# The last four expert tiles moved into three conditional blocks

## The chip, the cores and the metric

The kernel runs on one core of a Trainium2 chip. The metric is the device time of one execution in microseconds (us). A core has five engines that run side by side and wait for each other by semaphores: TensorE (PE in the profile; PEld is its weight loading), VectorE (DVE), ScalarE (ACT), GpSimd (POOL) and SyncE (SP). SP mostly issues transfers (DMA) here.

## The reference

Two things are computed, one after the other. First a Fourier filter along the sequence of 8 batches, then a mixture of 8 experts in which the token's number decides the expert:

```python
# x: (8, 2496, 256) float32; filt_r, filt_i: (1249, 256)
X = np.fft.rfft(x, axis=1)
y = np.fft.irfft(X * (filt_r + 1j * filt_i)[None], n=2496, axis=1)

x = y.reshape(19968, 256)
expert_idx = token_ids * np.int64(2654435761) % np.int64(8)
for e in range(8):
    mask = expert_idx == e
    h = np.maximum(x[mask] @ w1[e], 0.0)      # w1[e]: 256 x 1024
    out[mask] = h @ w2[e]                      # w2[e]: 1024 x 256
```

Everything is float32. The inputs are drawn from a fixed seed; the token numbers are drawn evenly from 0 to 49999.

## The kernel before

The tokens are sorted by expert into tiles of 128 rows, each tile of one expert. A tile that an expert doesn't fill is padded with blank rows. How many tiles are needed depends on the data: the sum over the experts of the number of tokens, divided by 128 and rounded up. The kernel is written for the worst case, 163 tiles, and always runs all of them; tiles beyond the needed number hold blank rows alone, and their results are scattered to a row index out of range, which drops them.

```python
TB = 128
NT = (N + E * (TB - 1)) // TB          # 163
STAGES = (2, 4, 6, 8)                  # a tile of stage g needs the filter's output of the first STAGES[g] batches

def stage_tiles():
    ends = [(S * b - E * (TB - 1)) // TB // 2 * 2 for b in STAGES[:-1]] + [NT]   # 30, 70, 108, 163
    out, first = [], 0
    for end in ends:
        half = (end - first + 1) // 2
        out.append([first + i // 2 + (half if i % 2 else 0) for i in range(end - first)])
        first = end
    return out
```

A stage's tiles are run alternately from its first and from its second half, so that the even steps use one pair of weight buffers and the odd steps the other. The weights of step i+2 are asked for in step i; the transfer is conditional (`cond`) on the expert being another than two steps before:

```python
    def weights(i, which):
        if i >= NT:
            return
        if i >= 2 and which == 0:
            ws[i] = ws[i - 2]
        eng, kw = nc.gpsimd if i < 2 else nc.sync, {}
        e = eng.value_load(chunk_i[0:1, 0, i:i + 1], ...)
        if i >= 2:
            kw = {"cond": eng.value_load(chunk_i[0:1, 1, i:i + 1], ...)}
        # which 0: w1 of expert e, 1 MB, into ws[i][0]; which 1: w2, 1 MB, into ws[i][1]
        eng.dma_start(..., **kw)
```

`rv["last"]` is the running sum of the tiles made, by stage and expert; its last element is the number of tiles that are needed. The expert of each tile and the flag of a change are worked out in `experts()` and left in `chunk_i`.

The main loop, with the pieces that it calls:

```python
    xps = pool(ctx, "xps", 1, PSUM)         # one buffer for the transposes
    work = pool(ctx, "work", 2)
    outs = pool(ctx, "outs", 3)

    def turn(i):                            # transposes of tile i's rows
        ps = xps.tile([P, DP, TB], F32, ...)
        for dp in range(DP):                # 2
            nc.tensor.transpose(out=ps[:, dp, :], in_=xg[i][:, dp * P:(dp + 1) * P], identity=ident[:])
        xt[i] = work.tile([P, DP, TB], F32, ...)
        nc.vector.tensor_copy(out=xt[i][:], in_=ps[:])

    def up(i, ht):                          # 16 matmuls 128x128x128, relu on ACT (quad 0) and DVE (quad 1)
        ...
    def down(i, ht):                        # 8 matmuls 128x128x256, then:
        ...
        o = outs.tile([P, C], F32, name=f"osb_{i}", tag="osb")
        nc.vector.tensor_copy(out=o[:], in_=ps[:])
        st = nc.gpsimd.indirect_dma_start(  # scatter of the tile's rows to out
            out=out[:], out_offset=..., in_=o[:], in_offset=None, bounds_check=N - 1, oob_is_err=False)

    for i in range(4):
        load(i)                             # gather buffer xg[i] <- xs
    turn(0)
    for i in range(NT):
        ht = work.tile([P, FP, TB], F32, name=f"ht_{i}", tag="ht")
        if i + 4 < NT:
            load(i + 4)
        up(i, ht)
        weights(i + 2, 0)
        if i + 1 < NT:
            turn(i + 1)
        while main and main[0][0] < i + 1:  # pieces of the filter for the later batches, up to step 101
            main.pop(0)[1]()
        down(i, ht)
        weights(i + 2, 1)
```

Of the kernel before, what the change touches and what calls it, by code (L numbers as in the profile page):

```python
# [11 lines left out]
F32 = mybir.dt.float32  # L12
I32 = mybir.dt.int32
# [6 lines left out]
P = 128  # L20
B, S, C = 8, 2496, 256
N = B * S
E, F = 8, 1024
# [19 lines left out]
TB = 128  # L43
NT = (N + E * (TB - 1)) // TB
W = C + 16
NJ = N // P
DP = C // P
FP = F // P
STAGES = (2, 4, 6, 8)
G = len(STAGES)  # L50
NPAD = NT * TB - N
NQP = NPAD // P


def stage_tiles():


    ends = [(S * b - E * (TB - 1)) // TB // 2 * 2 for b in STAGES[:-1]] + [NT]
    out, first = [], 0
    for end in ends:  # L60
        half = (end - first + 1) // 2
        out.append([first + i // 2 + (half if i % 2 else 0) for i in range(end - first)])
        first = end
    return out


# [30 lines left out]
def route_table():  # L97


    t = np.zeros((P, G + 2 + NQP + HN + 1), np.float32)  # L100
    p = np.arange(P)
    r = np.arange(NR)
    t[:NR, G + 2 + NQP:] = (N2 * (r % N1) + np.array(H0)[r // N1])[:, None] + np.arange(HN + 1)
    for g, b in enumerate(STAGES):
        t[:, g] = p < b * S // NJ
    order = sum(stage_tiles(), []) + [NT] * (2 * P - NT)
    t[:, G:G + 2] = np.array(order).reshape(2, P).T
    t[:, G + 2:G + 2 + NQP] = p[:, None] * NQP + np.arange(NQP)
    return t
# [3 lines left out]
def kernel(  # L113
# [10 lines left out]
    nc = tc.nc  # L124
# [9 lines left out]
    def pool(stack, name, bufs, space=None):  # L134
        kw = {} if space is None else {"space": space}
        return stack.enter_context(tc.tile_pool(name=name, bufs=bufs, **kw))

    ctx.enter_context(tc.manual_schedule())
    keep = pool(ctx, "keep", 1)
# [4 lines left out]
    t2pool = pool(ctx, "t2", 4)  # L144
# [10 lines left out]
    sidx = keep.tile([NR, B, HN + 1], I32)  # L155
    tokno = keep.tile([NR, HN + 1], F32)
    chunk_i = keep.tile([1, 2, NT], I32)
    wf_t = cpool.tile([NR, NK], F32)
    wi_t = cpool.tile([NK, NR], F32)
    d_t = cpool.tile([P, NS, P], F32)  # L160
# [153 lines left out]
# [7 lines that stand above are left out]
        e = eng.value_load(chunk_i[0:1, 0, i:i + 1], min_val=0, max_val=E - 1)  # L321
        if i >= 2:
            kw = {"cond": eng.value_load(chunk_i[0:1, 1, i:i + 1], min_val=0, max_val=1)}
        if which == 0:
            eng.dma_start(out=ws[i][0][:], in_=moe_w1[bass.ds(e, 1)].rearrange("one (dp p) f -> p (one dp) f", p=P), **kw)
        else:
            eng.dma_start(out=ws[i][1][:], in_=moe_w2[bass.ds(e, 1)].rearrange("one (fp p) d -> p (one fp) d", p=P), **kw)
# [9 lines left out]
    nc.scalar.dma_start(tok[:], tok_h.bitcast(I32).rearrange("(p j two) -> p j two", p=P, two=2))  # L337
    rt = rpool.tile([P, G + 2 + NQP + HN + 1], F32)
    nc.scalar.dma_start(out=rt[:], in_=r_dram.ap())
    nc.vector.tensor_copy(tokno[:], rt[0:NR, G + 2 + NQP:])  # L340

# [47 lines left out]
    rv = {}  # L389
# [111 lines left out]
    def blanks():  # L501
# [10 lines left out]
        nc.vector.tensor_sub(prior[:], prior[:], pads[:])  # L512
        some = rpool.tile([P, NQP, E], F32)
        number = rt[:, G + 2:G + 2 + NQP]
# [16 lines left out]
    def experts():  # L531
        seg = rv["seg"]
        ps = fps.tile([P, 2, C], F32, name="ce_ps", tag="f")
        for q in range(2):
            nc.tensor.matmul(out=ps[0:1, 0, q * P:(q + 1) * P], lhsT=seg[:, q:q + 1], rhs=ident[:],
                             start=True, stop=True)
        ce = rpool.tile([1, 2 * P], F32)
        nc.vector.tensor_copy(ce[:], ps[0:1, 0, :])
        new = rpool.tile([1, NT], F32)
        nc.vector.memset(new[:, 0:2], 1.0)  # L540
        nc.vector.tensor_tensor(new[:, 2:], ce[:, 2:NT], ce[:, 0:NT - 2], op=OP.not_equal)
        nc.vector.tensor_copy(chunk_i[:, 0, :], ce[:, 0:NT])
        nc.vector.tensor_copy(chunk_i[:, 1, :], new[:])

# [15 lines left out]
    def part3(b, at, ready):  # L562
        bt = batches[b]
        return ([(at[u], lambda u=u: bt.stage3(u)) for u in range(NU)] +
                [(max(at[2 * v] - 2.5 * (at[1] - at[0]), ready), lambda v=v: bt.load4(v)) for v in range(NV)])

    order = stage_tiles()
    tiles = sum(order, [])
    stage_of = [g for g, o in enumerate(order) for _ in o]
# [8 lines left out]
    todo += part2(0, spaced(-128, -95, N_2), -142)  # L578
    todo += part1(1, spaced(-123.5, -105, NU), [-141.5, -135, -134.5])
    todo += [(-125, tile_experts), (-121, experts), (-108, blanks)]  # L580
    todo += [(-110, lambda: nc.sync.dma_start(out=wi_t[:], in_=wi_dram.ap()))]
    todo += [(-118.2 + .1 * i, lambda i=i: (weights(i, 0), weights(i, 1))) for i in range(2)]
# [21 lines left out]
    work = pool(ctx, "work", 2)  # L604
    outs = pool(ctx, "outs", 3)
    xg, xt = {}, {}

    def load(i):
        q = tiles[i]
        xg[i] = gath.tile([P, W], F32, name=f"xg_{i}", tag="xg")  # L610
        ld = nc.sync.dma_start(out=xg[i][:], in_=xs[q * TB:(q + 1) * TB, :])
        for b in range(STAGES[stage_of[i]], B):
            tc.declare_no_dep(ld.ins, group=f"xs_{b}", reason="the tiles of a stage hold tokens of its batches alone")
        tc.add_to_no_dep_group("xs_read", ld.ins)

    def turn(i):
        ps = xps.tile([P, DP, TB], F32, name=f"xps_{i}", tag="xps")
        for dp in range(DP):
            nc.tensor.transpose(out=ps[:, dp, :], in_=xg[i][:, dp * P:(dp + 1) * P], identity=ident[:])  # L619
        xt[i] = work.tile([P, DP, TB], F32, name=f"xt_{i}", tag="xt")  # L620
        nc.vector.tensor_copy(out=xt[i][:], in_=ps[:])  # L621

    def up(i, ht):
        w1 = ws[i][0]
        for quad in range(FP // 4):
            ps = ups.tile([P, 4, TB], F32, name=f"ups_{i}_{quad}", tag="ups")
            for k in range(4):
                fp = 4 * quad + k
                for dp in range(DP):
                    nc.tensor.matmul(out=ps[:, k, :], lhsT=w1[:, dp, fp * P:(fp + 1) * P],  # L630
                                     rhs=xt[i][:, dp, :], start=(dp == 0), stop=(dp == DP - 1))
            dst = ht[:, 4 * quad:4 * quad + 4, :]
            if quad % 2 == 0:
                nc.scalar.activation(out=dst, in_=ps[:], func=AF.Relu)  # L634
            else:
                nc.vector.tensor_scalar_max(dst, ps[:], 0.0)  # L636

    def down(i, ht):
        w2 = ws[i][1]
        ps = dps.tile([P, C], F32, name=f"dps_{i}", tag="dps")  # L640
        for fp in range(FP):
            nc.tensor.matmul(out=ps[:], lhsT=ht[:, fp, :], rhs=w2[:, fp, :],  # L642
                             start=(fp == 0), stop=(fp == FP - 1))
        o = outs.tile([P, C], F32, name=f"osb_{i}", tag="osb")
        nc.vector.tensor_copy(out=o[:], in_=ps[:])  # L645
        st = nc.gpsimd.indirect_dma_start(  # L646
            out=out[:], out_offset=bass.IndirectOffsetOnAxis(ap=xg[i][:, C:C + 1].bitcast(I32), axis=0),
            in_=o[:], in_offset=None, bounds_check=N - 1, oob_is_err=False)
        tc.declare_no_dep(st.ins, group="out_rows", reason="distinct rows")
        tc.add_to_no_dep_group("out_rows", st.ins)  # L650
        del xg[i]

    for i in range(4):
        load(i)
    turn(0)
    for i in range(NT):
        ht = work.tile([P, FP, TB], F32, name=f"ht_{i}", tag="ht")
        if i + 4 < NT:
            load(i + 4)
        up(i, ht)  # L660
        weights(i + 2, 0)
        if i + 1 < NT:
            turn(i + 1)
        while main and main[0][0] < i + 1:
            main.pop(0)[1]()
        down(i, ht)
        weights(i + 2, 1)
    assert not main


# [26 lines left out]
```

## Time and profile before

The time before is 1637.09 us, the median of three runs (1634.4 to 1637.64). The profiled execution took 1631.37 us, and its recorded span is 1629.8 us.

| stretch of the span, us | PE busy, us | DVE busy, us | POOL busy, us | DMA share |
|---|---|---|---|---|
| 0 to 400 | 309.02 | 178.42 | 102.79 | 0.70 |
| 400 to 700 | 293.81 | 113.93 | 73.00 | 0.66 |
| 700 to 1000 | 297.26 | 116.79 | 73.32 | 0.55 |
| 1000 to 1300 | 298.13 | 66.11 | 62.85 | 0.40 |
| 1300 to 1500 | 200.00 | 39.52 | 27.20 | 0.25 |
| 1500 to 1620 | 120.00 | 23.86 | 15.54 | 0.20 |
| 1620 to 1630 | 0.58 | 0.42 | 0.97 | 0.03 |

How to read it: each row is one stretch of time. Where an engine's busy time equals the length of the stretch, it had no gap. DMA share is the mean busy share of the core's 16 DMA engines. The first matmul of the expert tiles starts at 207.7 us, the last at 1620.2 us; between about 208 and 1100 us the filter of the later batches is worked in between the tiles, and after that the tiles run alone.

### The profile page before, as it was taken

Reading aid. Unit: us, or ns where it says so; the run is one execution under the profiler, and the core shown is the slowest. Engines: PE = TensorE matmul, PEld = TensorE weight load, DVE = VectorE, ACT = ScalarE, POOL = GpSimd, SP = SyncE. Lnnn points to the kernel's source line nnn. Section 1 sums busy time; section 2 is a strip of 40 time slices with the busy share of each in tenths; the row PEclk is TensorE's granted clock in tenths of the full one; section 3 lists DMA queues with packets and bytes.
Section 4 is the critical chain, followed back from the end, with each engine's and each line's share of the span. In section 5 each row is a group of like instructions: output and inputs, shape, how many; then the busy total and the mean of one; then the engine's idle time right before and its main releaser. Section 6 shows DMA issues by size and latency. Waiting matters only on the chain.

```text
span 1629.8 us, 26685 instructions
## 1 busy us (share of the span) xinstructions
PE 1518.8 (93%) x9522; PEld 1381.7 (85%) x9522; DVE 539.0 (33%) x1022; ACT 217.1 (13%) x371; POOL 355.7 (22%) x375
## 2 busy tenths in 40 slices
PE   3676589999999999999999999999999999999997
PEld 2554378988888999899989998999999999999997
DVE  6572142452244444233434442222122121221221
ACT  2322212112111111111111111000000000000000
POOL 0235300331320132122121322233111111111111
PEclk9788699999999999999999999999999999999999
DMA  7998627747864883674537643544152413132220
GB/s 189 306 290 244 198 98 205 240 165 207 245 218 150 244 256 111 194 197 147 185 114 222 199 135 115 147 127 162 45 203 79 140 37 126 52 94 88 84 84 9
DMA packets 152541, 258.77 MB, mean 159 GB/s; under 512 B 16185, under 2 KB 118508, under 8 KB 150410
## 3 DMA queue, kind: packets, MB, share of 16 engines
q1 hardware_dynamic: 103345, 163.46, 33.1%
q0 software_dynamic: 21136, 50.96, 9.4%
q10 hardware_dynamic: 27928, 42.65, 8.3%
q8 instruction: 76, 1.25, 0.3%
q14 instruction: 56, 0.45, 0.1%
HBM read 431.87 MB, written 86.09 MB: 318 GB/s over the span
## 4 chain that ended last, share of the span: by engine, by line
PE 42%; issue 36%; POOL 7%; DMA 3%; DVE 2%; POOLq 1%; ACT 0%; SPq 0%; ACTq 0%; DVEq 0%
PE ups L630 15%; PE dps L642 15%; POOL out_dram L646 6%; PE pb L240 3%; PE pa L203 3%; PE pc L263 3%; PE pd L203 2%; POOL xs L301 2%; DMA xs<-o,sidx 1%; PE xps L619 1%; DVE z L250 1%; PE pa L198 0%; POOLq L646 0%; DMA d<-g 0%; DVE y L247 0%
## 5 line engine op out<-in xcount | busy, mean ns | idle before, releaser
L630 PEld LDWEIGHTS ups<-xt,w 128*128 128x128 f32 x5216 | 610.3, 193 | 9.2 <-DVE xt L621 1.0
L630 PE MATMUL ups<-xt,w 128*128 128x128 f32 x5216 | 611.1, 276 | 0.6 <-DVE xt L621 0.6
L642 PE MATMUL dps<-w,ht 128*128 128x256 f32 x2608 | 591.0, 380 | 0.0
L642 PEld LDWEIGHTS dps<-w,ht 128*128 128x128 f32 x2608 | 490.0, 191 | 63.7 <-issue 1.6
L646 POOL DMA_INDIRECT out_dram<-osb,xg x163 | 159.6, 979 | 944.6 <-DVE osb L645 919.4
L636 DVE TENSOR_SCALAR ht<-ups 128x512 f32<-128x512 f32 x163 | 112.8, 692 | 526.8 <-PE ups L630 519.7
L634 ACT ACTIVATE ht<-ups 128x512 f32<-128x512 f32 x163 | 97.3, 597 | 1008.0 <-PE ups L630 992.3
L301 POOL DMA_INDIRECT xs<-o,sidx x176 | 175.3, 996 | 245.7 <-DVE o L205 145.7
L645 DVE COPY osb<-dps 128x256 f32<-128x256 f32 x163 | 69.3, 425 | 404.5 <-PE dps L642 396.2
L240 PE MATMUL pb<-t,d_t 128*128 128x256 f32 x320 | 91.1, 413 | 23.8 <-DMA t<-d 23.3
L250 DVE TENSOR_TENSOR z<-pb,filt 64x512 f32<-64x512 f32 x160 | 110.1, 688 | 2.2
L263 PE MATMUL pc<-y,e_t 128*128 128x256 f32 x320 | 90.1, 407 | 19.7 <-DVE y L251 19.3
L240 PEld LDWEIGHTS pb<-t,d_t 128*128 128x128 f32 x320 | 63.5, 209 | 35.5 <-issue 25.9
L263 PEld LDWEIGHTS pc<-y,e_t 128*128 128x128 f32 x320 | 63.3, 203 | 35.8 <-issue 17.5
L203 PE MATMUL pd<-t,wi_t 120*117 120x256 f32 x320 | 81.2, 399 | 11.7 <-DMA t<-d 7.1
L203 PEld LDWEIGHTS pd<-t,wi_t 120*117 120x117 f32 x320 | 58.9, 191 | 25.5 <-issue 9.1
L247 DVE TENSOR_TENSOR y<-pb,filt 128x512 f32<-128x512 f32 x80 | 55.3, 691 | 68.3 <-PE pb L240 67.8
L266 ACT COPY g<-pc 128x512 f32<-128x512 f32 x80 | 46.8, 585 | 233.2 <-PE pc L263 229.8
L621 DVE COPY xt<-xps 128x256 f32<-128x256 f32 x163 | 67.6, 415 | 1.9 <-PE xps L619 1.9
L619 PE MATMUL xps<-ident,xg 128*128 128x128 f32 x326 | 62.6, 274 | 3.1 <-DMA xg<-xs 3.1
L203 PE MATMUL pa<-x,wf_t 117*120 117x256 f32 x264 | 63.3, 383 | 0.6 <-DVE z L250 0.6
L205 ACT COPY t<-pa 120x512 f32<-120x512 f32 x80 | 46.0, 588 | 90.6 <-PE pa L203 88.1
(102 smaller groups left out, 352.5 us busy)
## 6 DMA issues: line engine op xcount, KB each, us to landing
w<-in_moe_w_dram SPq DMA_DIRECT2D x322, 1024.0 KB
xg<-xs SPq DMA_DIRECT2D x163, 136.0 KB
t<-d SPq DMA_DIRECT2D x80, 256.0 KB
d<-g ACTq DMA_DIRECT2D x80, 256.0 KB
d<-t ACTq DMA_DIRECT2D x16, 960.0 KB
t<-d SPq DMA_DIRECT2D x16, 960.0 KB
x<-in_x_dram SPq DMA_DIRECT2D x39, 312.0 KB
x<-in_x_dram SPq DMA_DIRECT2D x21, 234.0 KB
```

The costliest lines, as they stand in the source:

```text
L203: nc.tensor.matmul(out=ps[0:cols * H, k, :], lhsT=w[:], rhs=src[:, 2 * i + k, :], start=True, stop=True)
L240: nc.tensor.matmul(out=ps[:, i, :], lhsT=d_t[:, s, :], rhs=self.t2[s // SG][:, s % SG, :], start=True, stop=True)
L250: nc.vector.tensor_tensor(out=z[b], in0=ps[a], in1=f_t[1][a, sl, :], op=OP.mult)
L263: nc.tensor.matmul(out=ps[:, i, :], lhsT=e_t[:, 2 * u + i, :], rhs=pr[:, i, :], start=True, stop=True)
L301: st = nc.gpsimd.indirect_dma_start(out=xs[:], out_offset=bass.IndirectOffsetOnAxis(ap=index, axis=0), in_=rows, in_offset=None, bounds_ch ...
L619: nc.tensor.transpose(out=ps[:, dp, :], in_=xg[i][:, dp * P:(dp + 1) * P], identity=ident[:])
L630: nc.tensor.matmul(out=ps[:, k, :], lhsT=w1[:, dp, fp * P:(fp + 1) * P], rhs=xt[i][:, dp, :], start=(dp == 0), stop=(dp == DP - 1))
L634: nc.scalar.activation(out=dst, in_=ps[:], func=AF.Relu)
L636: nc.vector.tensor_scalar_max(dst, ps[:], 0.0)
L642: nc.tensor.matmul(out=ps[:], lhsT=ht[:, fp, :], rhs=w2[:, fp, :], start=(fp == 0), stop=(fp == FP - 1))
L645: nc.vector.tensor_copy(out=o[:], in_=ps[:])
L646: st = nc.gpsimd.indirect_dma_start(out=out[:], out_offset=bass.IndirectOffsetOnAxis(ap=xg[i][:, C:C + 1].bitcast(I32), axis=0), in_=o[:], ...
```

## The change

The number of needed tiles is copied into an integer and loaded into a register of every engine in step 151. The last four tiles (159 to 162) are taken out of the alternating order of the last stage and stand at its end. Their transposes are done unconditionally, into one buffer of their own (`spare`, in a pool of the filter that is free by then). The rest of their work stands in three conditional blocks: tile 159, tile 160, and tiles 161 with 162, each block run only if more tiles are needed than its first tile's number. The change is for leaving out tiles that hold nothing but blanks.

```diff
+NSURE = NT - 4
...
-    ends = [(S * b - E * (TB - 1)) // TB // 2 * 2 for b in STAGES[:-1]] + [NT]
+    ends = [(S * b - E * (TB - 1)) // TB // 2 * 2 for b in STAGES[:-1]] + [NSURE]
     out, first = [], 0
     ...
+    out[-1] += range(NSURE, NT)
     return out
...
+    used_i = keep.tile([1, 1], I32)
...
         nc.vector.tensor_copy(chunk_i[:, 1, :], new[:])
+        nc.vector.tensor_copy(used_i[:], rv["last"][0:1, G * E - 1:])
...
-    def turn(i):
+    def turn(i, to=None):
...
-        xt[i] = work.tile([P, DP, TB], F32, name=f"xt_{i}", tag="xt")
-        nc.vector.tensor_copy(out=xt[i][:], in_=ps[:])
+        xt[i] = work.tile([P, DP, TB], F32, name=f"xt_{i}", tag="xt")[:] if to is None else to
+        nc.vector.tensor_copy(out=xt[i], in_=ps[:])
...
-    for i in range(NT):
+    used = []
+
+    def step(i):
         ht = work.tile([P, FP, TB], F32, name=f"ht_{i}", tag="ht")
         if i + 4 < NT:
             load(i + 4)
         up(i, ht)
         weights(i + 2, 0)
-        if i + 1 < NT:
+        if i + 1 < NSURE:
             turn(i + 1)
         while main and main[0][0] < i + 1:
             main.pop(0)[1]()
         down(i, ht)
         weights(i + 2, 1)
+
+    for i in range(NSURE):
+        if i == NSURE - 8:
+            used.append(nc.values_load(used_i[0:1, 0:1], min_val=0, max_val=NT))
+        step(i)
     assert not main
+
+    spare = t2pool.tile([P, NT - NSURE, DP, TB], F32, name="spare", tag="t2")
+    for i in range(NSURE, NT):
+        turn(i, spare[:, i - NSURE])
+    for some in (range(NSURE, NSURE + 1), range(NSURE + 1, NSURE + 2), range(NSURE + 2, NT)):
+        with tc.If(used[0] > some[0]):
+            for i in some:
+                ht = work.tile([P, FP, TB], F32, name=f"ht_{i}", tag="ht")
+                up(i, ht)
+                weights(i + 2, 0)
+                down(i, ht)
+                weights(i + 2, 1)
```

## The prediction

> **What bounds the kernel now.** I read the page's shares and slices first, then its groups, then the timeline of the last tiles, and last the tail, by the instructions of the kernel's closing line. From the page:
>
> ```profile
> PE 1518.8 (93%) x9522; PEld 1381.7 (85%) x9522; DVE 539.0 (33%) x1022; ACT 217.1 (13%) x371; POOL 355.7 (22%) x375
> ...
> L630 PE MATMUL ups<-xt,w 128*128 128x128 f32 x5216 | 611.1, 276 | 0.6 <-DVE xt L621 0.6
> L642 PE MATMUL dps<-w,ht 128*128 128x256 f32 x2608 | 591.0, 380 | 0.0
> ```
>
> TensorE is the bound: 93% of the span, and the two groups of the expert tiles have waited 0.6 us in all. 5216 / 163 = 32 and 2608 / 163 = 16 matmul records a tile. The chain of waits runs through POOL and "issue" at the end, but only because POOL's scatter comes last in every tile; it waits for TensorE each time. The timeline of one late tile shows what a tile costs:
>
> ```profile
> 1606.15 3.73 PE L630 MATMUL ups<-xt,w 128*128 128x128 f32 x32
> ...
> 1609.72 0.38 PE L619 MATMUL xps<-ident,xg 128*128 128x128 f32 x2
> ...
> 1609.93 3.62 PE L642 MATMUL dps<-w,ht 128*128 128x256 f32 x16
> 1609.98 0.69 DVE L636 TENSOR_SCALAR ht<-ups 128x512 f32<-128x512 f32 x1 [3.20 <-PE ups L630]
> 1610.58 0.41 DVE L621 COPY xt<-xps 128x256 f32<-128x256 f32 x1
> ...
> 1613.39 3.73 PE L630 MATMUL ups<-xt,w 128*128 128x128 f32 x32
> ...
> 1616.96 3.62 PE L642 MATMUL dps<-w,ht 128*128 128x256 f32 x16
> ...
> 1620.62 0.42 DVE L645 COPY osb<-dps 128x256 f32<-128x256 f32 x1 [2.71 <-PE dps L642]
> 1621.32 0.97 POOL L646 DMA_INDIRECT out_dram<-osb,xg  x1 [6.05 <-DVE osb L645]
> ```
>
> The columns are start and duration. From one tile's up matmuls to the next it is 1613.39 - 1606.15 = 7.24 us; over seven tiles (from 1562.68 to 1613.39) 50.71 / 7 = 7.244 us. The last matmul ends at 1616.96 + 3.62 = 1620.58; I call this moment T. The span ends at 1629.8, so the tail is 9.2 us. What fills it is among the instructions of the closing line:
>
> ```profile
> L692 SPq EVENT_SEMAPHORE  x12: 17/28/13964, 1606.5 to 1629.7; - x12
> ...
> L692 POOLq DRAIN  x3: 46/104/7897, 1621.1 to 1629.5; - x3
> L692 SPq DRAIN  x3: 7/7/13, 1624.0 to 1629.2; - x3
> ```
>
> (least, median and greatest duration in ns, first and last start.) SP has seen the last scatter land by 1624.0 = T+3.4. POOL's drain starts at 1621.1 and takes 7.9 us, to 1629.0 = T+8.4; then 0.8 us of barrier. So POOL's drain after its last scatter sets the end, and everything that is done by T+8.4 on other engines is free.
>
> **How many tiles are needed.** This decides everything. The inputs are fixed by the seed, so I counted: the experts get 2528, 2484, 2463, 2527, 2423, 2545, 2498 and 2500 tokens, in tiles 20, 20, 20, 20, 19, 20, 20, 20, together 159. The conditions are 159 > 159, > 160 and > 161: all three blocks are skipped.
>
> [...] No instruction of the profile before shows a conditional branch. [...] its queue of instructions moved 76 packets, 1.25 MB, 16 KB each, one about every 19 us; none has stalled TensorE late in the kernel, which was busy 200.00 of 200 us from 1300 to 1500. What a jump costs is not to be seen there.
>
> **The change part by part.**
>
> 1. Four tiles fewer on TensorE. The matmul stream before T is the same stream with four whole tiles less (192 records; the transposes of tiles 159 to 162 come after T now): 4 x 7.244 = 29.0 us off T. No engine waits between, so the whole of it is on the path: -29.0.
>
> 2. The register load in step 151, on all five engines. SP's loads of this kind (the flags of the weights) took 266 ns in the middle, 1127 ns at most. It stands in TensorE's stream ahead of a tile's up matmuls, where matmuls issued earlier may still cover it. Estimate from SP's durations: +0.5 (0 to 1.1). On the other engines it falls into idle time.
>
> 3. The new order of the last stage. I worked out the experts of all steps in both orders: the flag of a new expert is set in 39 steps before and 41 after. The odd steps now cross from expert 3 to 4 at step 113, after one at step 109; each needs 2 MB with four tiles (29 us) in between. How long a load takes is seen in the windows for step 155, whose two weight transfers were issued at 1551.95 and 1555.63:
>
> ```profile
> 1555.00:1556.00 1.00, 1.00 (x9) 0.95 (x8) 0.37 (x1) 0.00 (x0) 0.00 (x0) 1.00 1.04 430
> 1560.00:1561.00 1.00, 1.00 (x7) 0.87 (x6) 0.29 (x1) 0.00 (x0) 0.00 (x0) 1.00 1.03 366
> 1561.00:1562.00 1.00, 1.00 (x6) 0.90 (x5) 0.00 (x0) 0.00 (x0) 0.00 (x0) 1.00 0.08 28
> ```
>
> (the last two numbers are DMA share and GB/s.) The second had landed by about 1561.1, 5.5 us after its issue; a load has over 10 us before its use. Nothing: 0. The other extra loads are those of tiles 159 and 160, asked for in steps 157 and 158 outside the blocks, 4 MB that nobody uses. The last of them waits for tile 158's down matmuls, so it starts at T and lands at about T+5.5. SP waits for it at the end, but T+5.5 is ahead of T+8.4: 0.
>
> 4. Four pairs of transposes after T. With one PSUM buffer they go in turn: 0.38 us of PE, 0.41 us of copy and about 0.1 to 0.2 us of handing over, an estimate from these rows, make 4 x 0.95 = 3.8 us, done by about T+4. Ahead of T+8.4: 0. The scatter of tile 158 doesn't wait for them: DVE copies tile 158's result first.
>
> 5. The branches. A skipped block is, on each engine, a compare-and-branch, a wait and an add that make up for the semaphore counts of the work left out, and a jump. [...] On PE, ACT, DVE and SP this lies before T+8.4. On POOL it stands between the last scatter and the drain, with three extra instructions that add to the counts of its own DMA queue. If the drain keeps its length from the scatter, nothing is added; if its 7.9 us start anew after the branches, about 2 us. I take +1.5.
>
> Sum: -29.0 + 0.5 + 1.5 = -27.0, and 1637.1 - 27.0 = 1610.1; I say 1610.5.
>
> **The rivals.** (a) The tail grows by more: [...] extra instructions that POOL's software works off slowly. For it: the drain shows that POOL is slow after a scatter, and an instruction packet takes 0.9 to 1.7 us even without others in its way, while here 2 MB of weights are on the move at the same time. [...] It would make 1614 to 1619. (b) The register load empties TensorE's queue, or the new order of experts exposes a weight load: each would show as a gap of one to five us in PE: 1611 to 1615. Against it: nothing exposes a load before, at the same spacing. (c) The blocks are not skipped, or not cheaper than the work: 1640 or more. Against it: the count of 159. (d) The gain is greater than 29 us: I see no work for it, the most that can be left out is four tiles; it would need a shorter tail, and POOL's drain would have to shrink.
>
> **Range and chances.** The 29.0 is firm to some tenths. What is open is the tail (0 to +6) and the runs' own spread (1634.4 to 1637.6 before). That gives 1605.5 to 1616.5. Faster by over 2% would take 32.7 us, more than the four tiles: 0.02. Slower by over 2% needs something that I don't see at all: 0.01. Within 2%: 0.97.
>
> **What would show it.** 9522 - 192 = 9330 PE matmul records, with ups x5088, dps x2544 and xps still x326; 159 scatters to out; some 4.2 MB more on the queue of the weights. The last down matmul should end near 1620.6 - 28.5 = 1592, and PE should be without gaps from 1300 on but for at most 1 us near step 151 (about 1533). The span should end some 9 to 12 us after the last down matmul, with the transposes within 4 us and POOL's drain last. I am wrong if the tail is over 14 us, if PE has gaps at steps 109 to 116, if the drain is not what ends last, or if tiles 159 to 162 run.

## The result, and the profile after

The changed kernel takes 1614.15 us, the median of four runs (1611.64 to 1617.26), against 1637.37 us for the kernel before on the same chip (four runs, 1634.4 to 1637.74). The ratio is 0.9863, with a 95% interval of 0.9841 to 0.9885: 1.4% faster, inside the 2% that counts as the same.

The page of the changed kernel's profile, its shares and its costliest groups:

```profile
PE 1488.8 (92%) x9330; PEld 1351.5 (84%) x9330; DVE 534.6 (33%) x1015; ACT 215.1 (13%) x367; POOL 353.6 (22%) x371
...
q1 hardware_dynamic: 105969, 167.66, 34.8%
...
L635 PE MATMUL ups<-xt,w 128*128 128x128 f32 x5088 | 595.5, 275 | 0.6 <-DVE xt L626 0.6
...
L647 PE MATMUL dps<-w,ht 128*128 128x256 f32 x2544 | 579.7, 381 | 0.0
...
L651 POOL DMA_INDIRECT out_dram<-osb,xg x159 | 155.7, 979 | 920.3 <-DVE osb L650 887.3
```

The counts are those of 159 tiles: 9522 - 9330 = 192 matmul records less, 159 scatters. The queue of the weights (q1) moved 167.66 MB where it had moved 163.46, by its line in the profile before: the 4.2 MB more are the weights of tiles 159 and 160, which nobody uses.

```profile
q1 hardware_dynamic: 103345, 163.46, 33.1%
```

The timeline of the end (start, duration, engine, line, names):

```profile
1592.94 3.62 PE L647 MATMUL dps<-w,ht 128*128 128x256 f32 x16
...
1596.40 0.38 PE L624 MATMUL xps<-ident,xg 128*128 128x128 f32 x2
1596.60 0.37 SPq L331 DMA_DIRECT2D w<-in_moe_w_dram  x1
1596.60 0.42 DVE L650 COPY osb<-dps 128x256 f32<-128x256 f32 x1 [2.71 <-PE dps L647]
1597.00 0.42 DVE L626 COPY spare<-xps 128x256 f32<-128x256 f32 x1
1597.30 0.97 POOL L651 DMA_INDIRECT out_dram<-osb,xg  x1 [6.05 <-DVE osb L650]
...
1599.39 0.69 PE L624 MATMUL xps<-ident,xg 128*128 128x128 f32 x2 [0.52 <-DVE spare L626]
1600.12 0.42 DVE L626 COPY spare<-xps 128x256 f32<-128x256 f32 x1 [0.78 <-PE xps L624]
```

The last down matmul ends at T = 1592.94 + 3.62 = 1596.56, and the transposes are done at 1600.54 = T+4.0, as worked out. But the span ends at 1610.0 (1610.05 in the trace): the tail after T is 13.5 us, and it was 9.2. The instructions of the line of the conditional blocks, and those of the closing line, say why (least, median and greatest duration in ns, first and last start):

```profile
L686 POOLq COMPARE_BRANCH  x3: 45/45/54, 1597.1 to 1600.9; - x3
L686 POOLq INC_SWDGE_SEM  x3: 1686/1687/1729, 1597.3 to 1601.2; - x3
L686 PEldq COMPARE_BRANCH  x3: 221/236/446, 1599.4 to 1600.9; - x3
```

```profile
L716 POOLq DRAIN  x3: 46/103/6351, 1602.9 to 1609.8; - x3
L716 SPq DRAIN  x3: 7/7/13, 1603.5 to 1609.5; - x3
```

GpSimd passes each skipped block with an INC_SWDGE_SEM. By its name and its place I take it for what makes up the semaphore counts of the scatters that were left out: with all blocks run (e5, below) there is none on this line. On the other engines the line holds, beside the COMPARE_BRANCH, only EVENT_SEMAPHORE of 17 to 51 ns, and no jump of its own. There is one INC_SWDGE_SEM for each block, also for the last, which leaves out two scatters. Each takes 1.7 us, and they start 1.95 us apart; the branches themselves take 0.05 us. The three end at 1602.9 = T+6.3. Only then does GpSimd's drain begin, and it takes 6.35 us, to 1609.2 = T+12.7. The other engines are done by T+6.9, where SP's first drain starts.

### The profile page after: what moved, and what is told of

The parts are those of the page before. It is cut to its first block, busy times and chain, and to the rows that moved or that the text cites. A ratio compares the mean times of both kernels' runs of the same rounds, so it can differ in the third digit from the quotient of the medians.

```text
span 1610.0 us, 26261 instructions
## 1 busy us (share of the span) xinstructions
PE 1488.8 (92%) x9330; PEld 1351.5 (84%) x9330; DVE 534.6 (33%) x1015; ACT 215.1 (13%) x367; POOL 353.6 (22%) x371
## 3 DMA queue, kind: packets, MB, share of 16 engines
q1 hardware_dynamic: 105969, 167.66, 34.8%
## 4 chain that ended last, share of the span: by engine, by line
PE 86%; DMA 8%; DVE 3%; issue 1%; SPq 1%; ACT 1%; ACTq 0%; POOL 0%; DVEq 0%; POOLq 0%
PE ups L635 35%; PE dps L647 34%; PE pd L207 4%; PE pb L244 3%; PE pc L267 3%; PE pa L207 3%; DMA d<-t 3%; PE xps L624 2%; DMA t<-d 2%; DVE z L254 1%; DMA xs<-o,sidx 1%; DMA w<-in_x_dram 1%; DMA d<-g 1%; DVE y L251 1%; PE pa L202 0%
## 5 line engine op out<-in xcount | busy, mean ns | idle before, releaser
L635 PEld LDWEIGHTS ups<-xt,w 128*128 128x128 f32 x5088 | 594.7, 192 | 9.0 <-DVE xt L626 0.8
L635 PE MATMUL ups<-xt,w 128*128 128x128 f32 x5088 | 595.5, 275 | 0.6 <-DVE xt L626 0.6
L647 PE MATMUL dps<-w,ht 128*128 128x256 f32 x2544 | 579.7, 381 | 0.0
L647 PEld LDWEIGHTS dps<-w,ht 128*128 128x128 f32 x2544 | 479.3, 191 | 64.5 <-issue 1.8
L651 POOL DMA_INDIRECT out_dram<-osb,xg x159 | 155.7, 979 | 920.3 <-DVE osb L650 887.3
L267 PE MATMUL pc<-y,e_t 128*128 128x256 f32 x320 | 87.2, 396 | 20.2 <-DVE y L255 19.8
```

Of the source, the lines that this page charges most:

```text
L267: nc.tensor.matmul(out=ps[:, i, :], lhsT=e_t[:, 2 * u + i, :], rhs=pr[:, i, :], start=True, stop=True)
L651: st = nc.gpsimd.indirect_dma_start(out=out[:], out_offset=bass.IndirectOffsetOnAxis(ap=xg[i][:, C:C + 1].bitcast(I32), axis=0), in_=o[:], ...
```

## Where the gain went: one sum for two profiles

The 23.2 us of the medians and the 19.8 us between the two profiles (1629.8 - 1610.0) are less than the 29.0 us of four tiles. I cut both spans at two moments: the start of the scatter of step 108, from where on the tiles run alone, and T.

| part of the span, us | before | after | difference |
|---|---|---|---|
| start to the scatter of step 108 | 1230.3 | 1235.3 | +5.0 |
| from there to T | 390.27 | 361.29 | -28.98 |
| tail, T to the end | 9.20 | 13.49 | +4.29 |

The middle part is four tiles to the hundredth: 4 x 7.244 = 28.98. The tail takes 4.3 us back. The first part is the puzzle: the same work but for one copy of 4 bytes, 5 us longer.

## The experiments

Theory A: the tail is longer because GpSimd runs its INC_SWDGE_SEM for left-out scatters between its last scatter and its drain. Rival B: the transposes, the jumps or the unused weights set it. For the first part, theory L: the new buffer of 4 bytes moves nearly every later buffer by 32 bytes (the first of them from address 19136 to 19168), and this slows transfers. Rival N: the first part differs that much from run to run anyway. Each ratio below is to runs of the kernel before on the same chip.

| kernel | to the scatter of step 108 | from there to T | tail | ratio, 95% interval |
|---|---|---|---|---|
| before | 1230.3 | 390.27 | 9.20 | |
| after | 1235.3 | 361.29 | 13.49 | 0.9863, 0.9841 to 0.9885 |
| e1_one_block | 1237.3 | 361.29 | 10.77 | 0.9846, 0.9826 to 0.9867 |
| e2_no_shift | 1232.8 | 361.29 | 13.49 | 0.9878, 0.986 to 0.9895 |
| e3_before_used | 1236.6 | 390.27 | 9.20 | 1.0007, 0.9995 to 1.0019 |
| e4_159_only | 1237.3 | 361.29 | 8.88 | 0.9848, 0.9826 to 0.987 |
| e5_all_taken | 1239.4 | 392.66 | 9.23 | 1.0017, 1.0006 to 1.0028 |
| e6_no_last_scatter | 1239.6 | 361.29 | 1.77 | one run |
| e7_four_blocks | 1238.0 | 361.29 | 15.30 | one run |
| e8_nested_early | 1243.4 | 361.29 | 10.67 | 0.9858, 0.9833 to 0.9883 |
| e9_early_no_loads | 1238.3 | 361.29 | 8.90 | 0.9829, 0.9805 to 0.9854 |
| e10_three_no_loads | 1238.4 | 361.29 | 13.48 | one run |
| e11_one_no_loads | 1241.9 | 361.29 | 9.80 | 0.9832, 0.9803 to 0.9861 |
| e12_early_taken | 1242.8 | 393.09 | 10.51 | 1.0035, 1.0024 to 1.0045 |

The profiles come from several chips. Where the work is the same, the last two parts repeat to some hundredths, while the first wanders over 13 us. So the two parts of one profile answer here what medians of whole runs can't.

### One block, four blocks, none

```diff
 e1  -    for some in (range(NSURE, NSURE + 1), range(NSURE + 1, NSURE + 2), range(NSURE + 2, NT)):
     +    for some in (range(NSURE, NT),):
 e7  +    for some in [range(k, k + 1) for k in range(NSURE, NT)]:
 e4  register load, blocks, transposes, gathers and weights of tiles 159 to 162 taken out
```

> The changed kernel with its three conditional blocks made into one (tiles 159 to 162, run if more than 159 tiles are needed). Theory A, the three INC_SWDGE_SEM of 1.69 us that GpSimd works off between its last scatter and its drain make the tail longer: only one is left, so the tail from the last down matmul to the end of the span goes from 13.4 to about 10.0 us, 3.4 us less, and the time to about 1610.8. Rival B, the tail is set by the four transposes, the jumps or the unused weight loads: the same 13.4 us.

> The changed kernel with a block for each of the four tiles. Theory A: one INC_SWDGE_SEM more, so the tail goes from 13.5 to about 15.4 us (the three start 1.94 us apart). Rival B, something that comes once: 13.5 us.

> Only 159 tiles are run, with nothing decided on the chip: no register load, no conditional block, no transposes, gathers or weights of the last four tiles (the buffer of 4 bytes stays). It is right for these inputs alone. It is the floor for the change. If the register load and the new order cost nothing and the tail is the blocks' doing: a tail of 9.2 us as in the kernel before, so about 4.2 us below the changed kernel's 1614, 1610. If it still has a tail of 13 us, the blocks are not the cause.

Four blocks give 15.30 us, three 13.49, none 8.88: 1.8 us for the fourth, as theory A has it, and the one block is the exception. The drain and the instructions before it, with one block:

```profile
L686 POOLq INC_SWDGE_SEM  x1: 1745/1745/1745, 1599.4 to 1599.4; - x1
...
L716 POOLq DRAIN  x3: 46/103/7330, 1601.2 to 1609.1; - x3
```

and with four:

```profile
L686 POOLq INC_SWDGE_SEM  x4: 1675/1686/1724, 1600.0 to 1605.8; - x4
...
L716 POOLq DRAIN  x3: 46/103/6351, 1607.5 to 1614.4; - x3
```

With three and with four blocks the drain takes 6.351 us to the nanosecond; with one block it takes 7.33, and the tail is 10.8 instead of the 10.0 that I had expected. Something else holds the drain once GpSimd comes to it early. e8 to e11 look for it. The one INC_SWDGE_SEM stands here for four scatters and takes hardly longer, 1.745 us: what counts is the number of blocks passed, not that of the scatters left out.

### Is it the blocks when they are run?

```diff
-        nc.vector.tensor_copy(used_i[:], rv["last"][0:1, G * E - 1:])
+        nc.vector.tensor_scalar(used_i[:], rv["last"][0:1, G * E - 1:], 4.0, None, op0=OP.add)
```

> The changed kernel with 4 added to the number of needed tiles, so that all three blocks are run and all 163 tiles with them, as would happen on other data. Theory A says that what makes the changed kernel's tail longer is GpSimd's making up for left-out scatters; none is left out here, so the tail after the last down matmul is that of the kernel before, 9.2 us. The four transposes are no longer hidden behind other work (4 x 0.95 us) and TensorE passes three branches (0.2 to 0.4 us each): some 4 to 6 us more than the kernel before ahead of the last matmul, ratio about 1.003. Rival: the jumps and branches themselves lengthen the tail, then it is 13 us here too and the ratio 1.006.

The tail is 9.23 us with all three blocks run, so neither the branches nor the jumps lengthen it; leaving scatters out does. The part ahead of T grew by 392.66 - 390.27 = 2.4 us, half of what I expected. I had forgotten that a tile without transposes between its up and its down matmuls is shorter, 7.02 us against 7.24, and so by 0.9 us for four. The rest is that TensorE stood 3.1 us for the transposes ahead of tile 159, not 3.8, and that its branches left no gap that shows: the tiles in the blocks follow each other in 7.02 us:

```profile
1610.84 3.73 PE L635 MATMUL ups<-spare,w 128*128 128x128 f32 x32
...
1617.86 3.73 PE L635 MATMUL ups<-spare,w 128*128 128x128 f32 x32
```

This is also what the change costs on data that need all 163 tiles: 0.2%.

### Is it GpSimd's drain that ends the kernel?

```diff
 # from e4_159_only: the scatter of tile 158 is left out
+        if i == NSURE - 1:
+            return
         st = nc.gpsimd.indirect_dma_start(
```

> The kernel of 159 tiles without conditional blocks, and without the scatter of its last tile: 128 rows of the output are left unwritten. Theory D, GpSimd's drain takes its 7 to 8 us from its last scatter on and that alone sets the tail: the last scatter is now one tile (7.24 us) earlier, the drain ends about T+1, and the tail from the last down matmul shrinks from 8.9 to about 2 us. Rival: the drain or the barrier takes that long at the end of any kernel: the tail stays between 7 and 9 us.

The tail falls to 1.77 us. The last scatter that is left, the copy of the last tile, and the drain:

```profile
1594.59 0.97 POOL L653 DMA_INDIRECT out_dram<-osb,xg  x1 [6.27 <-DVE osb L650]
...
1600.92 0.42 DVE L650 COPY osb<-dps 128x256 f32<-128x256 f32 x1 [2.71 <-PE dps L647]
```

```profile
L705 POOLq DRAIN  x3: 46/104/7490, 1594.4 to 1602.4; - x3
```

The drain takes 7.49 us, about as long as in e4 (7.57), but it stands behind a scatter that is one tile earlier, and most of it lies beside the last tile's matmuls. So some 7 us of the tail of e4 are GpSimd's drain behind its last scatter. The kernel before has the same scatter and a drain of 7.9 us at its end; its scatter has landed 2.7 us after T, by the packets of its queue in the trace, 5.7 us before the drain ends.

### The first part of the span

```diff
 e2: used_i in the padding behind chunk_i
-    chunk_i = keep.tile([1, 2, NT], I32)
-    used_i = keep.tile([1, 1], I32)
+    chunk_u = keep.tile([1, 2 * NT + 1], I32)
+    chunk_i = chunk_u[:, 0:2 * NT].rearrange("p (k n) -> p k n", k=2)
+    used_i = chunk_u[:, 2 * NT:]
 e3: the kernel before, with
+    used_i = keep.tile([1, 1], I32)
+        nc.vector.tensor_copy(used_i[:], rv["last"][0:1, G * E - 1:])
```

> The changed kernel with the number of needed tiles stored in the padding behind chunk_i, so that no buffer that comes after moves; in the changed kernel the new buffer of 4 bytes moves nearly all others on the chip by 32 bytes. Theory L, the move of 32 bytes makes transfers or engines slower and is why the changed kernel loses 4.8 us of its gain in the first 500 us: the scatter of tile 25 starts near 499 instead of 504 us, the last down matmul ends near 1591.8, and the time is 4 to 5 us below the changed kernel's. Rival N, the first 500 us differ from run to run by such amounts: no difference beyond the noise of a few us.

> The kernel before with the new buffer and the copy into it alone: nothing is loaded into registers, no tile is left out, the order is the old one. Theory L: slower than the kernel before by 4 to 5 us (about 1642, ratio 1.003), all of it in the first 500 us. Rival N: the same as before, ratio 1.000 within 0.001.

Theory L, 4 to 5 us, falls. The move of 32 bytes and the copy with nothing else give 1.0007 (0.9995 to 1.0019, 22 runs), so at most 0.2% or 3.1 us; and the kernel without the move is no faster than the changed one (1614.63 against 1614.15 us, on two chips; ratios 0.9878 and 0.9863). In the profiles the scatter of step 108 starts anywhere from 1230.3 to 1243.4 us, though the work up to there is the same, and 27 runs of the kernel before on one chip range from 1631.51 to 1642.18 us. The profile of the kernel before was an early one: that execution took 1631.37 us, less than all four timed runs (1634.4 at least). The two parts that repeat give 28.98 - 4.29 = 24.7 us, and the medians show 23.2.

Two things stay open. What moves the first part isn't known: over the 27 runs a longer time goes with a lower mean granted clock (correlation -0.67), but in the first 300 us of the two profiles the quicker one, that of the kernel before, has the lower clock (0.86 against 0.89). And in all ten kernels that were timed four times or more, the medians show 0.8 to 3.9 us less gain, or more loss, than the last two parts (e8: a gain of 23.6 us against 27.5). All ten have the copy of 4 bytes, so a loss of one to three us in the first part is not excluded.

### The drain with one block: the late scatter

```diff
 # e8_nested_early: conditions nested, transposes inside, tile 158's scatter after the blocks
+    def rest(k):
+        with tc.If(used[0] > parts[k][0]):
+            ...                                # turn, up, weights, down of the tiles of parts[k]
+            if k + 1 < len(parts):
+                rest(k + 1)
+    rest(0)
+    for i in held:                             # tile 158 alone, its result in a buffer of its own
+        scatter_out(i)
```

> The three conditions nested, so that only the outer one is passed when no tile is left to do, with the four transposes inside the blocks, and with the scatter of tile 158 put after the blocks in GpSimd's order (in a buffer of its own). GpSimd then passes the branch and its one INC_SWDGE_SEM while TensorE is still on tile 158. Theory A: the tail goes back to that of the kernel before, 9.2 us or a few tenths more, 4.2 us less than the changed kernel's and 1.5 less than with one block; the time is about 1609.5. If waits on other engines set the tail after all, it stays at 10.8.

A miss: 10.67 us instead of 9.2. GpSimd did its one INC_SWDGE_SEM at 1598.5, 6 us ahead of T = 1604.67, and yet the drain was longer than any, 9.34 us. Its scatter, SP's wait for it, and the windows of two us after T (the last two columns are DMA share and GB/s):

```profile
1605.41 0.97 POOL L659 DMA_INDIRECT out_dram<-osb,xg  x1 [6.05 <-DVEq L696]
```

```profile
SPq L734 <- DMA out_dram<-osb,xg: 5.2, 1, 5.2
```

```profile
1604.67:1606.67 2.00, 0.00 (x1) 0.00 (x0) 0.42 (x1) 0.00 (x0) 0.97 (x1) 1.00 0.80 280
1606.67:1608.67 2.00, 0.00 (x0) 0.00 (x0) 0.00 (x0) 0.00 (x0) 0.00 (x0) 0.54 1.00 303
1608.67:1610.67 2.00, 0.00 (x0) 0.00 (x0) 0.00 (x0) 0.00 (x0) 0.00 (x0) 0.50 0.71 251
```

The DMA engines are busy for 0.80, 1.00 and 0.71 of these windows, with the weights for tiles that don't run, and the last scatter is among them. By the packets of its queue in the trace it lands at T+6.2, against T+2.7 in the kernel before (after: T+5.8, one block: T+6.3). Theory W follows: with one block and in e8 the drain waits for the late scatter; it ended 3.7 us after the landing in both. (It also ended 4.0 us after the last packet of the unused weights in both, at T+6.0 and T+5.8. No run tells the two apart.) The test takes the unused weights away: it sets the flag of a new expert to zero for tiles that aren't needed:

```diff
+        need = rpool.tile([1, NT - NSURE], F32)
+        nc.vector.tensor_scalar(need[:], iota_e[0:1, 0:NT - NSURE], float(NSURE), None, op0=OP.add)
+        nc.vector.tensor_tensor(need[:], need[:], rv["last"][0:1, G * E - 1:].to_broadcast([1, NT - NSURE]), op=OP.is_lt)
+        nc.vector.tensor_tensor(new[:, NSURE:], new[:, NSURE:], need[:], op=OP.mult)
         nc.vector.tensor_copy(chunk_i[:, 0, :], ce[:, 0:NT])
```

> The kernel with nested conditions and the late scatter of tile 158 (e8_nested_early), with the flags that ask for new weights also set to zero for tiles that are not needed, so that the 4 MB for tiles 159 and 160 stay away. Theory W: in e8 the last scatter landed only about 6.2 us after the last down matmul, because the unused weights held the DMA engines up to 5.8 us after it, where it lands 2.7 us after it in the kernel before; the drain ends some 3.7 us after the landing. Without the loads the scatter lands by 2.9 us, the drain ends 6.4 to 6.7 us after the scatter's issue, and the tail is 9.2 us. If the tail stays at 10.7, the conditional block costs it in another way.

> The changed kernel with one block and without the unused weights. By the same reckoning: the one INC_SWDGE_SEM ends 2.6 us after the last down matmul, the drain takes 6.35 us from there, and 0.8 us of barrier follow: a tail of 9.8 us, against 10.8 with the loads. If it stays at 10.8, the loads are not what sets the tail with one block.

> The changed kernel with its three blocks, without the unused weights. Theory A, in this one the three INC_SWDGE_SEM and the drain behind them end later than what hangs on the late scatter: the tail stays at 13.5 us, within 0.3. If the unused weights delay the end here too, it falls to 12 or less.

The tails are 8.90, 9.80 and 13.48 us, where 9.2, 9.8 and 13.5 were expected. The windows of e9, whose T is 1599.62, and its drain:

```profile
1599.62:1601.62 2.00, 0.00 (x1) 0.00 (x0) 0.42 (x1) 0.00 (x0) 0.97 (x1) 1.00 0.01 4
1601.62:1603.62 2.00, 0.00 (x0) 0.00 (x0) 0.00 (x0) 0.00 (x0) 0.00 (x0) 0.68 0.18 66
```

```profile
L738 POOLq DRAIN  x3: 46/109/7570, 1600.1 to 1608.3; - x3
```

and the drain of e11, with its one INC_SWDGE_SEM still behind the scatter:

```profile
L720 POOLq DRAIN  x3: 46/103/6351, 1605.8 to 1612.7; - x3
```

The three INC_SWDGE_SEM of e10 take 1.69 to 1.72 us where they took 1.69 to 1.73 with the weights on the move, so those transfers don't hold them up:

```profile
L690 POOLq INC_SWDGE_SEM  x3: 1686/1687/1724, 1600.4 to 1604.3; - x3
```

So the drain's end fits two lower bounds, of which the later one counts: 6.35 us after GpSimd's last INC_SWDGE_SEM, or 6.3 to 6.7 us after the end of its last scatter's record; and some 3.7 us after a landing that the unused weights delay (seen in two kernels). What the drain does in this time the traces don't show. With three blocks behind the scatter the first rules, and the unused weights cost nothing (13.48 without them, 13.49 with them). With one block or none behind the scatter the second does, and they cost 1.0 us (10.77 to 9.80) and 1.8 us (10.67 to 8.90). e9 has nothing left of the cost of deciding on the chip: its tail is that of the kernel with 159 tiles fixed (8.90 and 8.88). Its parts after step 108 sum to 370.2 us, the changed kernel's to 374.8, the kernel before's to 399.5. In the medians, 0.9829 against 0.9863, the two intervals overlap.

> The kernel of e8_nested_early with 4 added to the number of needed tiles, so that all of its nested blocks are run. What it costs on data that need all 163 tiles: ahead of the last down matmul some 2 to 4 us more than the kernel before, as with the three blocks, and about 1 us more in the tail, since the scatter of tile 158 now comes after that of tile 162: ratio about 1.002.

The nested form costs more when its blocks are run: 2.8 us ahead of T and 1.3 in the tail, in sum 4.1, and a ratio of 1.0035. Each of the three blocks now begins with its own transposes, and TensorE stands 0.6 to 0.8 us for their copy. In the tail, tile 158's scatter comes after that of tile 162, at T+2.0 instead of T+0.7.

## Why the prediction was right

- The number of tiles, 159, and the 28.98 us of TensorE's time: as worked out, to the hundredth.
- The register load, taken as +0.5, cost nothing. TensorE's own load took 0.5 us in its sequencer and left no gap:

```profile
L678 PEldq TENSOR_LOAD <-used_i x1: 496/496/496, 1536.0 to 1536.0; - x1
```

```profile
1230.00:1533.00 303.00, 303.00 (x2091) 285.65 (x2090) 60.81 (x126) 24.48 (x41) 40.51 (x42) 1.00 0.28 89
1533.00:1545.00 12.00, 12.00 (x84) 11.30 (x83) 2.47 (x5) 1.19 (x2) 1.26 (x2) 1.00 0.65 210
```

  The number behind the comma is TensorE's busy time: 303.00 of 303 us and 12.00 of 12 us. The same windows clear the new order of experts (steps 109 to 116), so rival (b) is out.
- The transposes: done at T+4.0 and hidden, as said.
- The unused weights: they landed at T+5.9, and they don't set the end of the changed kernel, as said. But I looked at their landing alone; that the scatter's landing would move from T+2.7 to T+5.8 beside them I had not seen, and it shows as soon as GpSimd has fewer blocks to pass.
- The branches on GpSimd are the term that was mis-sized: +1.5 in the sum, an estimate of mine that no trace had shown, and 4.29 measured. I had put the danger in the right place, between the last scatter and the drain, and had the drain start anew at worst, but took the three extra instructions for tenths of a us: they are 1.7 us each, and the drain did start anew behind them, with 6.35 us. It is rival (a), the extra instructions that GpSimd works off slowly. The jumps themselves set nothing: from a branch's start to its engine's next instruction at most 0.6 us passed (on ScalarE, ahead of T; 0.2 on GpSimd), and no branch took more than 0.45 us (0.05 on GpSimd, 0.22 to 0.45 on TensorE).
- The sum: -29.0 + 0.5 + 1.5 = -27.0 foreseen, -28.98 + 0 + 4.29 = -24.7 found in the parts, -23.2 in the medians. The middle of the forecast, 1610.5, was 3.65 us too low. The tail of 13.5 us lies over the 9 to 12 that were foreseen and just under the 14 that were to show the prediction wrong, and 1614.15 us is the lower edge of what rival (a) was given. T came at 1596.56 instead of 1592, since the first part was 5 us longer in this profile. The range held it because it had been given 6 us for the tail.

## What to carry to other kernels

Leaving work out by a condition was worth its time on the engine that bounds this kernel, 28.98 us for four tiles, but the end of the kernel must be read on its own: the INC_SWDGE_SEM that GpSimd ran behind its last scatter were paid there, 0.9 us for the first skipped block (8.90 to 9.80) and 1.8 for each further one (9.80 to 13.48 for two, 13.49 to 15.30 for one). In this kernel it paid to put the blocks so that GpSimd passes them while TensorE still works, to give it one condition to pass and not several, and to prefetch nothing for what is left out: the tail fell from 13.49 to 8.90 us, though the whole times are too noisy to show it. Where the first part of a kernel varies from run to run, here from 1230.3 to 1243.4 us, compare the parts that repeat.

## What the runs showed of the hardware

- INC_SWDGE_SEM on GpSimd took 1.68 to 1.75 us each in the skipped blocks, for one left-out scatter or for four, 1.9 us from start to start. The one at the kernel's start took 0.03 us.
- GpSimd's drain at the end took 6.35 us behind such an instruction in four kernels (after, e7, e10, e11), and 7.33 with one block and the unused weights on the move (e1). Behind a scatter it ended 6.3 to 6.7 us after the scatter's record (before, e5, e6, e9), in the kernel before 5.7 us after its landing. With the last scatter one tile earlier, the tail was 1.77 instead of 8.88 us.
- A scatter of 128 KB issued while the unused weights were on the move landed 5.1 us (after) and 5.5 us (e8) after its issue, instead of 2.0 (before). The DMA share in the first four us after T was 0.98 and 1.00 in after, 0.80 and 1.00 in e8.
